# State times w_in of batches 4 to 7: from the first block into the second and third

## The chip, the cores and the metric

The kernel runs on one core of one Trainium2 chip. The metric is the device time of one execution in microseconds, the median of several runs. In the profile, PE is TensorE's matmuls, PEld its weight loads (which overlap the matmuls), DVE is VectorE, ACT is ScalarE, POOL is GpSimd, and SP is SyncE, which here only issues DMA transfers.

## The reference, cut to what matters

```python
def _attn_ref(x, state):                       # x 8 x 8 x 512 x 64, state 8 x 8 x 32 x 64
    a = softmax(scale * x @ state.T)           # over the 32 state rows
    xread = a @ state                          # 512 rows of each batch and head
    a2 = softmax(scale * state @ x.T)          # over the 512 tokens
    sread = a2 @ x                             # 32 rows of each batch and head
    return concat([xread, sread], axis=2)
# then, on 8 * 544 rows of 512 numbers:
h = x @ w_in                                   # 512 x 2048
x = max(0.01 * h, h) @ w_out                   # 2048 x 512
x = (silu(x @ w_gate) * (x @ w_val)) @ w_out2  # 512 x 1536, 1536 x 512
```

All in float32. The kernel gets the weights as 64-bit words (float64 bits) and converts them itself.

## The kernel before

**The trick of the first layer.** Since xread is a @ state, the product xread @ w_in is a @ (state @ w_in). The kernel therefore makes SW = state @ w_in once for every batch and head and multiplies the softmax weights a with it, which saves a step for the 512 token rows of a batch. The 32 sread rows of each batch are gathered in a "tail" that goes through w_in in the ordinary way at the end of the layer.

**Blocks and slots.** The first layer runs in eight blocks, one for each batch, of 16 slots each, one for each 128 columns of the hidden layer (variable `f`). The slots are numbered through: block j has slots 16 j to 16 j + 15. A steady slot has six matmuls into `ps_h` (`h_mm`, for the slot after next), the activation on ACT and DVE (`hs`, `gh`, `gl`), and twelve matmuls into four banks `ps_y` (`y_mm`). Every product of two float32 numbers is made from high and low parts in three passes (`passes`, line 443). After a block, `y_out` copies the four banks into one tile with the tag `yst` (128 x 4 x 512) and stores it.

**State times w_in before the change.** `product_sw(g, p, bs, banks)` makes, for column group g of w_in (4 of 512 columns), row group p (4 of 128 rows, two heads) and half bs of the batches (0 to 3, or 4 to 7), two matmuls over 64 rows each (line 467) into two banks. ACT copies each bank into a staging tile `sw` (line 475; two buffers for each of the two halves e) and SP stores it to `sw_dram` (line 476). There are 4 x 4 x 2 = 32 such calls, 64 matmuls (two records each in the trace), 64 copies and 64 stores of 256 KB. `load_sw` (line 494) loads the rows of one batch again, some slots before its block needs them, and `split_sw_h` and `split_sw_l` split them in high and low parts. Batch 0 alone is made straight from the banks (`state_win`, line 455, "keep").

**What sets the order in block 0.** Everything is issued in an order written out by hand: the string `START` ahead of slot 0, and one string of `SLOT0` for each slot of block 0. The letter `p` is one call of `product_sw` if some w_in piece is ready (`pump_products`, line 1187), `c` is one quarter of the conversion of one weight piece (`convert`: two ACT operations of lines 214 and 215, DVE operations of lines 216, 219, 222 and 225, one 512 KB load for the next piece; pieces of w_out are also split, lines 165 and 168, and pieces of w_in are stored in float32 to `win_dram`, line 232). `D`, `H`, `A`, `S`, `Y`, `L`, `Z` are the parts of the slot itself: H the matmuls into `ps_h`, Y and Z the two halves of `y_mm`. `finish1_h` forces products that are still open when the tile that holds their w_in piece is to be overwritten.

**Later blocks.** From slot 16 on, `put` lays each batch's softmax steps (`read_state`: scores into bank `a`; `read_tokens`: `turn` into bank `a`, `read` into bank `b`), the `load_sw` steps and the splits in the slots by their costs and due times. In a slot the parts run in the order W, D, matmuls, A, `y_mm`, and at last P and L of each step. The rest of a slot's vector time goes to `fill`, which converts the second layer's weights and stores their parts. Bank pool `ps_a` has one buffer for tag `a` and one for tag `b`. SP works through its DMAs in program order and waits at each one until its tile is free.

Of the kernel before, what the change touches and what calls it, by code (L numbers as in the profile page):

```python
# [9 lines left out]
F32 = mybir.dt.float32  # L10
# [15 lines left out]
def kernel(  # L26
# [46 lines left out]
    KD = DM // P  # L73
    NF1 = FF1 // P
    NF2 = FF2 // P
    NC = S // P
    NPAIR = H // 2
# [3 lines left out]
    FB = 4  # L81
# [6 lines left out]

    LOADS = "xswxxwww"
    ORDER = "iiiioiiooiioiioioiioioioiooooooo"  # L90
    START = "spc0Scpccc0p0cpccpcc1ccchcc1cccpc1clcpp0hcccpclp1c01cpcmcc"
    SLOT0 = [
        "DcHcpAccccSYLpcZccc",
        "DcHcAcccpSYLpccZccc",
        "DcHcpccAcSYLZccpp",
        "cDccHcApSccYLpcZcccc",
        "cDcHccApScYLcZpc",
        "cccDHpccAccScpYLccZ",
        "ccDcHAcpScccYcLZcp",
        "ccDccHcApSccpYcLcZ",  # L100
        "cDcHcpcApSYLcccZ",
        "ccDHcAScYcpLccZcp",
        "ccDcHcASYcpLccZcp",
        "cDHccASccYLcpcZ",
        "pcDHccASccYLcpcZ",
        "cpcDcHAccSYLccpccZp",
        "DcpcHcccpAcSYLcpZ",
        "pDpcHccpAcSYLcZp",
    ]
    KEEP = (0, 1, 3, 5, 8, 7)  # L110
    WS = 5

    Y_SUMS = 5

    WQ = 16

# [16 lines left out]
    first1 = layer1.enter_context(tc.tile_pool(name="first1", bufs=1))  # L133
    wsp = layer1.enter_context(tc.tile_pool(name="wsp", bufs=2))
    ab = layer1.enter_context(tc.tile_pool(name="ab", bufs=1))
    xin = layer1.enter_context(tc.tile_pool(name="xin", bufs=3))
# [9 lines left out]
    cv = first.enter_context(tc.tile_pool(name="cv", bufs=1))  # L146

    ident = const.tile([P, P], F32, name="ident")

    states = first1.tile([P, NPAIR, B, 2 * NS], F32, name="states")  # L150
    y_dram = [dram.tile([P, KD, widths[j]], F32, name=f"y_dram{j}") for j in range(NB)]
    win_dram = [dram.tile([P, KD, 512], F32, name=f"win_dram{g}") for g in range(FB)]

# [17 lines left out]
    xt, xn = {}, {}  # L171
# [18 lines left out]
    raw = {}  # L190
# [37 lines left out]
    ready = []  # L228
# [146 lines left out]
    def read_tokens(b, q):  # L375

        pairs = (2 * q, 2 * q + 1)
        v = {}

        def softmax_max():  # L380
            v["s"] = S_.pop((b, q))
            v["m2"] = at3.tile([P, 1], F32, tag="m2", name="m2")
            nc.vector.tensor_reduce(out=v["m2"], in_=v["s"], axis=AX.X, op=ALU.max)
            nc.vector.tensor_scalar(out=v["m2"], in0=v["m2"], scalar1=-SCALE, scalar2=None, op0=ALU.mult)

        def softmax_exp():
# [12 lines left out]
        def turn():  # L399
            ps = v["ps"] = ps_a.tile([P, 512], F32, tag="a", name="ps_a2")  # L400
            for c in range(NC):
                nc.tensor.transpose(ps[:, c * P:(c + 1) * P], v["e2"][:, c * P:(c + 1) * P], ident)

        def turned():
            v["et"] = at3.tile([P, 512], F32, tag="et", name="et")
            nc.scalar.copy(v["et"], v["ps"])

        def read():

            ps = v["ps"] = ps_a.tile([P, 2, NS], F32, tag="b", name="ps_r")  # L410
# [12 lines left out]
            next_xn(2)  # L423

        def read_out():
            nc.vector.tensor_copy(out=x_tail[:, pairs[0]:pairs[0] + 2, b * NS:(b + 1) * NS], in_=v["ps"])

        return [
            {"D": [softmax_max], "A": [softmax_exp], "cost": 0.8},
            {"D": [softmax_norm], "cost": 0.8},  # L430
            {"P": [turn], "L": [turned]},
            {"P": [read]},
            {"D": [read_out], "cost": 0.2},
        ]
# [14 lines left out]
    products = []  # L449
# [8 lines left out]
            )  # L458
        return ps

    def product_sw(g, p, bs, banks):

        pool = ps_y if banks == "yy" else ps_a
        ps = [pool.tile([P, 512], F32, tag=tag, name="ps_sw") for tag in banks]
        for e in range(2):
            half = slice(D * e, D * (e + 1))
            nc.tensor.matmul(  # L467
                ps[e], lhsT=flat[half, p, 4 * bs:4 * bs + 4, :].rearrange("d b n -> d (b n)"),
                rhs=raw["in", g, p][half], start=True, stop=True,
            )  # L470
        for e in range(2):

            pool, tag, bufs = ((cv, "sw", 2), (xin, "xn", 2))[e]
            t = pool.tile([P, 512], F32, tag=tag, name="sw", bufs=bufs)
            nc.scalar.copy(t, ps[e])  # L475
            nc.sync.dma_start(out=sw_dram[bs][g][2 * p + e], in_=t)

    def sw_tiles(b, g, q):
        SW[b, g, q] = tuple(wsp.tile([P, 512], F32R, tag="ab"[q] + t, name="sw" + t) for t in "hl")
# [8 lines left out]
        split_l(SW[0, g, q][1], sw_ps.pop((g, q)), SW[0, g, q][0])  # L488

    def load_sw(b, g, q):  # L490
        assert not any((g, p, b // 4) in products for p in (2 * q, 2 * q + 1))
        t = SW_raw[b, g, q] = xin.tile([P, 512], F32, tag="sw", name="sw")
        rows = slice(NS * (b % 4), NS * (b % 4 + 1))
        nc.sync.dma_start(
            out=t, in_=sw_dram[b // 4][g][4 * q:4 * q + 4, rows]
        )
# [8 lines left out]
    W = {}  # L505
# [500 lines left out]
    with tc.manual_schedule():  # L1006

        ins = [("in", g, k) for g in range(FB) for k in range(KD)]
        outs = [("out", f) for f in range(NF1)]
# [22 lines left out]
                raw[key] = cv.tile([P, 512], F32, tag="raw", name="raw", bufs=4)  # L1032

        def finish1_h(key):
            while any((KD * g + p) // 2 + NF1 // 2 == key[1] for g, p, _ in products):
                pump_products(1)
            t = wres.tile([P, 2, 512], F32R, tag=f"wr{key[1]}", name="w_parts")
            WO[key[1]] = (t[:, 0, :], t[:, 1, :])
            split_h(t[:, 0, :], raw[key])
# [84 lines left out]
        slots = {}  # L1124
# [7 lines left out]
        def put(start, steps, kind=None, behind=2):  # L1132


            at = []
            for k, step in enumerate(steps):
                slot = max([start] + [t + 1 for t in at[-1:] + before.get(kind, [])[k + behind:k + behind + 1]])
                cost = step.get("cost", 0)
                while k and "now" not in step and load.get(slot, 0) + cost > budget(slot):
                    slot += 1  # L1140
                load[slot] = load.get(slot, 0) + cost
                slots.setdefault(slot, []).append(step)
                at.append(slot)
            before[kind] = at
            return at

        def start_tokens(n):
            return NF1 + n * 11 // 2
# [18 lines left out]
        for g in range(1, FB):  # L1167
            for q in range(2):
                put(KEEP[2 * g - 2 + q], keep_steps(g, q), "keep")
        made = {0: 0, 1: 0}  # L1170

        for n in range(2, 2 * B):
            start = max((n // 2 - 1) * NF1 + EARLY + 6 * (n % 2), start_tokens(n - 4) + 1) if n > 3 else 6 * (n % 2)
# [1 line left out]
            made[n] = r[1] + 1  # L1175
            assert r[-1] < n // 2 * NF1 - 2, (n, r)
        for n in range(2 * B):
            put(max(start_tokens(n), made[n]), read_tokens(n // 2, n % 2), "tokens")

        def run(steps, part):  # L1180
            for step in steps:
                for op in step.get(part, ()):
                    op()

        products[:] = [(g, p, bs) for g in range(FB) for p in range(NPAIR) for bs in range(B // 4)]

        def pump_products(n, banks="ab"):
            for _ in range(n):
                one = next((one for one in products if ("in", *one[:2]) in ready), None)
                if one:  # L1190
                    products.remove(one)
                    product_sw(*one, banks)

        keep = [(0, 0), (0, 1)]
        low = list(keep)
# [2 lines left out]
        for action in LOADS:  # L1198
            if action == "w":
                next_load1()  # L1200
            elif action == "x":
                next_xt(1)
            else:
                nc.sync.dma_start(
                    out=flat.rearrange("p k b n -> p (k b n)"), in_=state_t.rearrange("e d k b n -> (e d) (k b n)")
                )
        nc.gpsimd.memset(states, 0.0)
        make_identity(nc, ident)

# [257 lines left out]
```

## Time and profile before

| | before |
|---|---|
| runs | 1481.33, 1483.01, 1483.09 us |
| median | 1483.01 us |
| profiled execution | 1480.25 us |
| its span | 1478.2 us |
| PE busy | 98% |
| PEld, DVE, ACT busy | 78%, 56%, 47% |
| HBM | 309.58 MB moved, 209 GB/s |
| block 0 ends (first copy of `yst`) | 155.35 us |
| first layer ends (last store of `yst`) | 702.7 us |

The profiled execution took 1480.25 us, 2.05 us more than its span and 2.76 us less than the median of the runs. The table is read from the top: PE is busy nearly always, and and the shares of the other engines are averages over stages with different limits: a first block in which the first layer's weights are converted and stored, seven blocks in which the second layer's are, and a second layer with no conversion. So the stretches are read apart below.

### The profile page before, as it was taken

To read this page: it belongs to the slowest core of one execution; us is meant where nothing else is said; L and a number is where in the kernel's file an instruction comes from. 1 tells how busy PE (TensorE), PEld (TensorE's weight loads), DVE (VectorE), ACT (ScalarE), POOL (GpSimd) and SP (SyncE) were. 2 spreads that over 40 slices of the span, in tenths; PEclk is the share of its full clock that TensorE was granted. 3 is DMA by queue.
4 is the path that set the end of the run, shared out by engine and by line. 5 is a ranking of instruction groups with operands and counts; after the bars stand their busy time and mean duration, and the time that the engine had idled before them with its cause. 6 is when DMAs were issued, how large, how long until landed. Compare 5 with 4: busy or idle time off the path is not lost.

```text
span 1478.2 us, 19617 instructions
## 1 busy us (share of the span) xinstructions
PE 1450.5 (98%) x7018; PEld 1159.7 (78%) x7018; DVE 829.4 (56%) x1460; ACT 688.2 (47%) x1242; POOL 3.0 (0%) x8
## 2 busy tenths in 40 slices
PE   5999999999999999999999999999999999999998
PEld 1545877878787878888888888888888878988887
DVE  5877677676767686243444535555344555644442
ACT  6877556655665666444333433334223333433322
POOL 0000000000000000000000000000000000000000
PEclk9999999999999999999999999999999999999999
DMA  8996556665655655260668676677666386876345
GB/s 296 317 321 217 186 206 214 206 223 191 228 214 198 207 189 200 90 208 21 215 194 280 229 233 203 193 220 244 232 193 193 104 309 228 266 255 193 119 150 191
DMA packets 146640, 309.58 MB, mean 209 GB/s; under 512 B 14064, under 2 KB 34544, under 8 KB 145520
## 3 DMA queue, kind: packets, MB, share of 16 engines
q1 hardware_dynamic: 145392, 299.95, 61.7%
q10 hardware_dynamic: 1152, 8.39, 1.4%
q8 instruction: 56, 0.92, 0.3%
q14 instruction: 40, 0.33, 0.1%
HBM read 231.74 MB, written 76.55 MB: 209 GB/s over the span
## 4 chain that ended last, share of the span: by engine, by line
PE 93%; DMA 3%; ACT 2%; DVE 1%; issue 1%; SPq 0%; ACTq 0%; DVEq 0%
PE ps_y L443 23%; PE ps_o L443 18%; PE ps_x L728 18%; PE ps_h L443 14%; PE ps_s L728 9%; PE ps_a L728 4%; PE ps_t L443 2%; PE ps_yt L443 2%; PE ps_sw L467 2%; PE ps_r L416 1%; PE ps_s L319 1%; DMA wo<-wo 1%; DMA wraw<-w_gate 1%; DMA sw_dram<-sw 1%; ACT sw L475 1%
## 5 line engine op out<-in xcount | busy, mean ns | idle before, releaser
L443 PE MATMUL ps_y<-gh,w_parts 128*128 128x512 f32 x1024 | 339.1, 391 | 0.0
L728 PE MATMUL ps_x<-yc,wq 128*128 128x512 f32 x1152 | 278.0, 389 | 0.0
L728 PEld LDWEIGHTS ps_x<-yc,wq 128*128 128x128 f32 x1152 | 216.2, 188 | 44.8
L443 PE MATMUL ps_o<-wo,zh 128*128 128x512 f32 x768 | 236.4, 389 | 0.0
L443 PEld LDWEIGHTS ps_y<-gh,w_parts 128*128 128x128 f32 x1024 | 192.2, 188 | 51.6 <-issue 7.6
L443 PE MATMUL ps_y<-gl,w_parts 128*128 128x512 f32 x512 | 199.3, 389 | 0.0
L168 DVE TENSOR_TENSOR gl<-hs,gh 128x512 fp32r<-128x512 f32 (+1 forms) x144 | 95.1, 660 | 146.9 <-ACT gh L165 146.7
L443 PEld LDWEIGHTS ps_o<-wo,zh 128*128 128x128 f32 x768 | 144.2, 188 | 30.0
L536 ACT ACTIVATE hs<-ps_h 128x512 f32<-128x512 f32 (+1 forms) x144 | 82.7, 575 | 180.2 <-PE ps_h L443 179.0
L443 PE MATMUL ps_o<-wo,zl 128*128 128x512 f32 x384 | 149.5, 389 | 2.0 <-DMA wo<-wo 2.0
L728 PE MATMUL ps_s<-yc,wq 128*128 128x512 f32 x576 | 146.1, 389 | 0.0
L168 DVE TENSOR_TENSOR zl<-z,zh 128x512 fp32r<-128x512 f32 x96 | 66.3, 691 | 117.4 <-ACT zh L165 117.4
L165 ACT CAST zh<-z 128x512 fp32r<-128x512 f32 x96 | 59.3, 621 | 143.6 <-PE ps_o L443 143.5
L728 PEld LDWEIGHTS ps_s<-yc,wq 128*128 128x128 f32 x576 | 108.1, 188 | 22.5
L748 ACT ACTIVATE sg<-C 128x512 f32<-128x512 f32 x72 | 45.5, 632 | 158.1 <-DVE C L744 158.1
L443 PEld LDWEIGHTS ps_y<-gl,w_parts 128*128 128x128 f32 x512 | 96.2, 188 | 19.6
L443 PE MATMUL ps_h<-ah,swl 128*128 128x512 f32 x256 | 106.6, 416 | 1.0 <-DVE swl L168 1.0
L744 DVE TENSOR_TENSOR C<-ps_s,C 128x512 f32<-128x512 f32 x48 | 33.2, 691 | 123.3 <-PE ps_s L728 123.3
L443 PE MATMUL ps_h<-al,swh 128*128 128x512 f32 x256 | 100.6, 393 | 0.1
L443 PE MATMUL ps_h<-ah,swh 128*128 128x512 f32 x256 | 100.7, 393 | 0.0
L740 ACT COPY C<-ps_x 128x512 f32<-128x512 f32 x96 | 56.1, 584 | 94.6 <-PE ps_x L728 93.8
L165 ACT CAST gh<-hs 128x512 fp32r<-128x512 f32 (+1 forms) x144 | 85.6, 595 | 3.0
(127 smaller groups left out, 1923.3 us busy)
## 6 DMA issues: line engine op xcount, KB each, us to landing
wo<-wo SPq DMA_DIRECT2D x96, 512.0 KB
wq<-quad_gate SPq DMA_DIRECT2D x168, 256.0 KB
wq<-quad_val SPq DMA_DIRECT2D x168, 256.0 KB
ws<-in_dram SPq DMA_DIRECT2D x68, 512.0 KB
sw_dram<-sw SPq DMA_DIRECT2D x64, 256.0 KB
sw<-sw_dram SPq DMA_DIRECT2D x56, 256.0 KB
quad_gate<-hl SPq DMA_DIRECT2D x24, 512.0 KB
quad_val<-hl SPq DMA_DIRECT2D x24, 512.0 KB
```

What stands on the lines that cost most here:

```text
L165: nc.scalar.copy(dst, src)
L168: nc.vector.tensor_tensor(out=dst, in0=src, in1=hi.bitcast(F32), op=ALU.subtract)
L319: nc.tensor.matmul(ps[2 * NS * i:2 * NS * (i + 1)], lhsT=states[:, p, b, :], rhs=xt.pop((b, p)), start=True, stop=True,)
L416: nc.tensor.matmul(ps[D * e:D * (e + 1), i], lhsT=tokens[i][:, c, D * e:D * (e + 1)], rhs=v["et"][:, n:n + NS], start=(c == 0), stop=(c == ...
L443: nc.tensor.matmul(ps, lhsT=w, rhs=v, start=first and n == 0, stop=last and n == len(todo) - 1)
L467: nc.tensor.matmul(ps[e], lhsT=flat[half, p, 4 * bs:4 * bs + 4, :].rearrange("d b n -> d (b n)"), rhs=raw["in", g, p][half], start=True, s ...
L475: nc.scalar.copy(t, ps[e])
L536: nc.scalar.activation(hs, ps[:, :n], AF.Prelu, alpha=0.01)
L728: nc.tensor.matmul(bank, lhsT=a, rhs=v, start=first and n == 0, stop=last and n == len(todo) - 1, skip_group_check=True,)
L740: nc.scalar.copy(t[0], src)
L744: nc.vector.tensor_tensor(out=kept[0], in0=bank, in1=kept[0], op=ALU.add)
L748: nc.scalar.activation(t[0], c, AF.Sigmoid)
```

## The change

Only the products of batches 0 to 3 stay in `START` and `SLOT0`: 16 of the 32 calls, and the letters `p` are thinned out accordingly (11 to 6 in `START`, 36 to 18 in `SLOT0`; the number of `c` is the same). The 16 products of batches 4 to 7 are made in eight rounds of two, four rounds in block 1 and four in block 2. A round takes three slots: in the first (part W) SP loads two 256 KB pieces of w_in from `win_dram` into a tile with the tag `yst`, the tile of the blocks' results; in the second and in the third slot one product each is made at the end of the slot (part P, ahead of the slot's other P steps, since it is inserted at place 0). ACT copies its two banks into the same tile, over the piece of w_in that was used, and SP stores from there. The rounds begin in slots 18, 21, 24, 27 and 34, 37, 40, 43. A new small tile `states1` holds the states of batches 4 to 7 and is loaded by one more DMA, issued from ACT, at the very start. (`held_b` comes out empty by the planner's own numbers, since `read_out` follows `read` in the next slot.)

```diff
-    def product_sw(g, p, bs, banks):
+    def product_sw(g, p, bs, banks, stationary, w, outs):
...
             nc.tensor.matmul(
-                ps[e], lhsT=flat[half, p, 4 * bs:4 * bs + 4, :].rearrange("d b n -> d (b n)"),
-                rhs=raw["in", g, p][half], start=True, stop=True,
+                ps[e], lhsT=stationary[half, p].rearrange("d b n -> d (b n)"), rhs=w[half], start=True, stop=True
             )
         for e in range(2):
...
+            t = outs(e)
             nc.scalar.copy(t, ps[e])
             nc.sync.dma_start(out=sw_dram[bs][g][2 * p + e], in_=t)
...
+    def later_sw(g, p):
+        v = {}
+        def begin():
+            v["t"] = ab.tile([P, KD, S], F32, tag="yst", name="later")
+            for i in range(2):
+                nc.sync.dma_start(out=v["t"][:, 2 * i, :], in_=win_dram[g][:, p + i, :])
+        def product(i):
+            product_sw(g, p + i, 1, "ab", states1, v["t"][:, 2 * i, :], lambda e: v["t"][:, 2 * i + e, :])
+        return [{"W": [begin]}, {"P": [lambda: product(0)]}, {"P": [lambda: product(1)]}]
...
+        for n in range(2 * FB):
+            slot = NF1 * (1 + n // 4) + LATER + 3 * (n % 4)
+            for step in later_sw(n // 2, 2 * (n % 2)):
+                while slot in held_b and "P" in step:
+                    slot += 1
+                slots.setdefault(slot, []).insert(0, step)
+                slot += 1
...
-        products[:] = [(g, p, bs) for g in range(FB) for p in range(NPAIR) for bs in range(B // 4)]
+        products[:] = [(g, p) for g in range(FB) for p in range(NPAIR)]
...
+        nc.scalar.dma_start(
+            out=states1.rearrange("p k b n -> p k (b n)"),
+            in_=state_t[:, :, :, 4:B, :].rearrange("e d k b n -> (e d) k (b n)"),
+        )
```

## Rows read from the trace of the kernel before

**Rows 1.** Windows: length, busy of PE, PEld, DVE, ACT, POOL; clock, DMA share, GB/s.

```profile
13.30:41.10 27.80, 23.49 (x58) 9.12 (x58) 22.26 (x44) 20.55 (x39) 0.00 (x0) 0.94 0.81 279
41.10:140.40 99.30, 93.27 (x344) 48.83 (x344) 81.01 (x154) 81.55 (x152) 0.00 (x0) 1.00 0.87 301
140.40:155.30 14.90, 14.90 (x67) 12.37 (x66) 4.76 (x8) 6.18 (x11) 0.00 (x0) 1.00 0.47 111
155.30:226.00 70.70, 70.70 (x376) 55.37 (x376) 49.41 (x99) 43.69 (x81) 0.00 (x0) 1.00 0.58 203
226.00:297.00 71.00, 71.00 (x393) 56.84 (x390) 50.60 (x104) 43.51 (x80) 0.00 (x0) 1.00 0.63 213
```

**Rows 2.** Chain that ended last, steady pieces: start us, us, what.

```profile
43.84 1.06 PE ps_sw L467 x4
44.90 1.59 PE ps_y L443 x6
...
170.36 0.44 PE ps_a L402 x4
...
174.90 1.06 PE ps_r L416 x32
...
184.34 1.36 PE ps_h L443 x6
185.70 2.72 PE ps_y L443 x12
```

**Rows 3.** Groups by line, 41.1 to 140.4: busy us, mean ns, idle before, releasers.

```profile
L467 PE MATMUL ps_sw<-w_in,flat 64*128 64x512 f32 x100 | 31.8, 641 | 4.3 <-ACT sw L475 4.3
L475 ACT COPY sw<-ps_sw 128x512 f32<-128x512 f32 x50 | 27.2, 591 | 6.7 <-PE ps_sw L467 3.7 <-DMA sw_dram<-sw 2.4 <-ACT hs L536 0.4
```

**Rows 4.** Waits of DVE, 41.1 to 140.4: us in total, times, longest.

```profile
DVE gl L168 <- ACT gh L165: 6.7, 4, 4.6
DVE w_in L216 <- ACT ws L214: 4.2, 4, 1.6
DVE swl L168 <- ACT swh L165: 3.6, 4, 1.5
```

**Rows 5.** Windows, two of the twelve slots 0 to 11; columns as in rows 1.

```profile
109.75:119.30 9.55, 8.37 (x33) 4.33 (x31) 4.20 (x8) 6.92 (x13) 0.00 (x0) 1.00 0.95 336
119.30:126.00 6.70, 6.70 (x29) 3.77 (x27) 6.70 (x14) 6.17 (x12) 0.00 (x0) 1.00 0.70 234
sum 104.40, PE 98.37 PEld 52.57 DVE 84.60 ACT 86.37 POOL 0.00; mean PE 8.20 PEld 4.38 DVE 7.05 ACT 7.20 POOL 0.00
```

**Rows 6.** Chain that ended last, DMA pieces: start us, us, what.

```profile
1.19 3.70 DMA flat<-in_dram
...
104.65 8.25 DMA sw_dram<-sw
```

**Rows 7.** Timeline of PE, 98 to 106: start, us, what [idle before <-releaser].

```profile
98.02 1.13 PE L467 MATMUL ps_sw<-w_in,flat 64*128 64x512 f32 x4
99.82 1.08 PE L319 MATMUL ps_s<-xt,states 128*64 128x512 f32 x4 [0.67 <-ACT sw L475]
...
102.43 1.13 PE L467 MATMUL ps_sw<-w_in,flat 64*128 64x512 f32 x4
104.23 1.61 PE L467 MATMUL ps_sw<-w_in,flat 64*128 64x512 f32 x4 [0.67 <-ACT sw L475]
105.77 0.50 PE L443 MATMUL ps_y<-gh,w_parts 128*128 128x512 f32 x1
```

**Rows 8.** Timeline of SP and ACT: a store and a reload, and who waited.

```profile
27.50 3.33 SPq L476 DMA_DIRECT2D sw_dram<-sw  x4
...
32.48 0.59 ACT L475 COPY sw<-ps_sw 128x512 f32<-128x512 f32 x1 [0.41 <-DMA sw_dram<-sw]
...
563.09 6.39 SPq L1260 DMA_DIRECT2D tail_in<-win_dram  x5
...
566.75 0.62 ACT L165 CAST ch<-tail_in 128x512 fp32r<-128x512 f32 x1 [2.19 <-DMA tail_in<-win_dram]
```

More of the change, by code (lines that the diff above doesn't have):

```diff
@@ L90 @@
     ORDER = "iiiioiiooiioiioioiioioioiooooooo"
-    START = "spc0Scpccc0p0cpccpcc1ccchcc1cccpc1clcpp0hcccpclp1c01cpcmcc"
+    START = "spc0Scccc0p0cccpcc1ccchcc1cccc1clcp0hcccpcl1c01cpcmcc"
     SLOT0 = [
[L93 to L103, printed above, removed]
+        "DcHcAccccSYLpcZccc",
+        "DcHcAcccSYLpccZccc",
+        "DcHcccAcSYLZccp",
+        "cDccHcApSccYLcZcccc",
+        "cDcHccApScYLcZc",
+        "cccDHpccAccScYLccZ",
+        "ccDcHAcpScccYcLZc",
+        "ccDccHcApSccYcLcZ",
+        "cDcHcpcASYLcccZ",
+        "ccDHcAScYcpLccZc",
+        "ccDcHcASYcpLccZc",
         "cDHccASccYLcpcZ",
[L105 to L108, printed above, removed]
+        "cDHccASccYLcpcZ",
+        "ccDcHAccSYLccpccZ",
+        "DcpcHcccAcSYLcpZ",
+        "DpcHccAcSYLcZp",
     ]
@@ L113 @@
     Y_SUMS = 5
+    LATER = 2
     WQ = 16
@@ L150 @@
     states = first1.tile([P, NPAIR, B, 2 * NS], F32, name="states")
+    states1 = first1.tile([P, NPAIR, B - 4, NS], F32, name="states1")
     y_dram = [dram.tile([P, KD, widths[j]], F32, name=f"y_dram{j}") for j in range(NB)]
@@ L467, in product_sw, with first_sw, staged_sw @@
             nc.tensor.matmul(
-                ps[e], lhsT=flat[half, p, 4 * bs:4 * bs + 4, :].rearrange("d b n -> d (b n)"),
-                rhs=raw["in", g, p][half], start=True, stop=True,
+                ps[e], lhsT=stationary[half, p].rearrange("d b n -> d (b n)"), rhs=w[half], start=True, stop=True
             )
         for e in range(2):
-            pool, tag, bufs = ((cv, "sw", 2), (xin, "xn", 2))[e]
-            t = pool.tile([P, 512], F32, tag=tag, name="sw", bufs=bufs)
+            t = outs(e)
             nc.scalar.copy(t, ps[e])
             nc.sync.dma_start(out=sw_dram[bs][g][2 * p + e], in_=t)
+    def first_sw(g, p, banks):
+        def staged_sw(e):
+            pool, tag, bufs = ((cv, "sw", 2), (xin, "xn", 2))[e]
+            return pool.tile([P, 512], F32, tag=tag, name="sw", bufs=bufs)
+        product_sw(g, p, 0, banks, flat[:, :, 0:4, :], raw["in", g, p], staged_sw)
+    def later_sw(g, p):
[7 more added lines that the diff above has]
+        return [{"W": [begin]}, {"P": [lambda: product(0)]}, {"P": [lambda: product(1)]}]
     def sw_tiles(b, g, q):
@@ L490, in load_sw @@
     def load_sw(b, g, q):
-        assert not any((g, p, b // 4) in products for p in (2 * q, 2 * q + 1))
+        assert b >= 4 or not any((g, p) in products for p in (2 * q, 2 * q + 1))
         t = SW_raw[b, g, q] = xin.tile([P, 512], F32, tag="sw", name="sw")
@@ L1034, in finish1_h @@
         def finish1_h(key):
-            while any((KD * g + p) // 2 + NF1 // 2 == key[1] for g, p, _ in products):
+            while any((KD * g + p) // 2 + NF1 // 2 == key[1] for g, p in products):
                 pump_products(1)
@@ L1169 @@
                 put(KEEP[2 * g - 2 + q], keep_steps(g, q), "keep")
-        made = {0: 0, 1: 0}
+        made, held_b = {0: 0, 1: 0}, set()
         for n in range(2, 2 * B):
@@ L1177 @@
         for n in range(2 * B):
-            put(max(start_tokens(n), made[n]), read_tokens(n // 2, n % 2), "tokens")
+            at = put(max(start_tokens(n), made[n]), read_tokens(n // 2, n % 2), "tokens")
+            held_b.update(range(at[3] + 1, at[4]))
+        for n in range(2 * FB):
[5 more added lines that the diff above has]
+                slot += 1
         def run(steps, part):
@@ L1183, in run @@
                     op()
-        products[:] = [(g, p, bs) for g in range(FB) for p in range(NPAIR) for bs in range(B // 4)]
+        products[:] = [(g, p) for g in range(FB) for p in range(NPAIR)]
         def pump_products(n, banks="ab"):
             for _ in range(n):
-                one = next((one for one in products if ("in", *one[:2]) in ready), None)
+                one = next((one for one in products if ("in", *one) in ready), None)
                 if one:
                     products.remove(one)
-                    product_sw(*one, banks)
+                    first_sw(*one, banks)
         keep = [(0, 0), (0, 1)]
```

## The prediction, made before the change was run

> **What bounds the kernel now.** I first cut the span in stretches, busy time of each engine [rows 1]. From 155.3 us on, in blocks 1 and 2, PE is busy in all of 70.7 and 71.0 us, with ACT at 62% and DMA at about 60%: whatever is added to PE there lengthens the span by its full time. Block 0 looks different: from 41.1 to 140.4 us, its slots 0 to 11, PE is busy 93.27 of 99.30 us, ACT 81.55, DVE 81.01, DMA 87%. Nothing is at its limit by itself, three are near. Then I read the chain of waits for the price of a product [rows 2], the groups by line for how many lie where [rows 3], and DVE's waits for how much of its idle time is the products' doing [rows 4]. Slots 12 to 15 (140.4 to 155.3 us) hold no product any more and run at PE's pace, so they don't change.
>
> **Products on PE.** In the chain one product (four records) takes 1.06 us, and the six matmuls after it 1.59 instead of the 1.36 that six take in the steady state [rows 2]: 1.06 + 0.22 = 1.28 us of PE for each. The sixteen products in blocks 1 and 2 therefore cost 16 x 1.28 = 20.5 us. In eight of the sixteen places another float32 step (scores, turn or read) follows in the same slot, and the 0.22 is paid there already: -1.8. Term: **+18.7 us**, bounds 17.0 (no 0.22 anywhere) to 20.5.
>
> **What block 0 gives back.** Of the 32 products 25 lie in slots 0 to 11 (100 records [rows 3]) and 7 before them, where PE waits for the first conversions anyway. After the change 4 fit in `START` by its letters and 12 in the slots: 13 fewer, or 13 x 1.28 = 16.6 us of PE, and the waits that ACT's copies cause, 4.3 us [rows 3], mostly go too. PE alone could give some 21 to 25 us. But the number of `c` is unchanged, and so is DVE's work: 84.6 us in the twelve windows of the slots from 36 us on, which last 104.4 us [rows 5]. So DVE is late next. I took for each slot the larger of DVE's busy time in its window and PE's new work (4.08 from rows 2, plus 1.28 for one product, plus 1.01 + 0.22 where a keep or scores step lies in it). That is DVE in eleven of the twelve (the last row with DVE at 6.70 of 6.70 us is one) and PE in slot 8 (9.55 us now, 6.6 then), and sums to 87.1. At 96%, a little under what DVE reaches in slot 9 alone, that is 90.7 us, 13.7 less than now. Term: **-14 us**. Bounds: -20 (DVE without any pause, 84.6) to -7: of DVE's 18.3 us of idle time in slots 0 to 11 the waits for `gh`, `ws` and `swh` are 14.5 [rows 4], and half of them, those on `swh` among them, are chains of PE, ACT and DVE that remain. What hides nothing here: the stores that go (16 products, 8.4 MB) free DMA, which isn't the bound then, and the 32 copies of 0.59 us [rows 3] free ACT, which has room by then.
>
> **The start.** The load of `states1` (256 KB) goes in beside the load of `flat`, 512 KB in 3.70 us, which ACT's first copy waits for [rows 6]. Half as much again could delay that by 0 to 1.9 us; three fewer products before 41 us take ACT's copies out of a stretch where DVE is busy 22.26 of 27.80 us [rows 1], a gain of 0 to 2. I take **+0.4 us**. Its issue on ACT lies in the time in which ACT waits for `flat`.
>
> **Waits for a bank.** A product takes banks `a` and `b` at the end of a slot, ahead of the slot's other P steps, and these need the same banks, of which there is one each. The trace has both cases [rows 7]: scores behind a product started 1.80 us after it instead of 1.06, so +0.74 for bank `a`; and a second product, whose second half needs `b`, took 1.54 instead of 1.06 on top, so +1.22 for `b`. Going through the plan by its costs and due times, a product stands ahead of scores or turn (`a`) in slots 22, 23, 28, 29 and 45 and ahead of read (`b`) in slots 19, 35 and 41. Term: 5 x 0.74 + 3 x 1.22 = **+7.4 us**, bounds 4 (copies that start at once) to 10 (ACT late by 0.3 us each time). Behind the waiting matmul PE's whole next slot is queued.
>
> **Waits for the reload.** The tile with tag `yst` has one buffer. So each round's two loads wait on SP until the four stores of the round before have landed, and the second product's stores are issued only at the end of the slot just before. From the start of a second product at t: the copies end and the store is issued at t + 2.2 (102.43 to 104.65 [rows 6, 7]); a 256 KB store of this kind landed 4.9 us after its issue (27.50 to 32.44, by the copy that waited [rows 8]), in another place 8.25 [rows 6]; a 256 KB load from the very same `win_dram` took 3.7 (563.09 to 566.75 [rows 8]). The next product can start at t + 2.2 + 4.9 + 0.1 + 3.7 = t + 10.9. PE is there at t + 1.28 + 2 x 4.08 = t + 9.4, later where P steps lie between (turn 0.44, scores 1.2, read 1.3 [rows 2]). For the six rounds that follow on another in their block that gives waits of 1.5, 0, 1.5, 1.5, 1.0 and 0.2. Term: **+5.7 us**. Bounds: 0.6 (a store as fast as the load, 3.7) to 24.8 (8.25 for the store). I take 4.9, since DMA is at 60% in blocks 1 and 2 against 81% in the stretch of the 4.9 [rows 1]; the 8.25 fell where it was at 87%.
>
> By the Trainium skill, DMA: Bandwidth & Descriptors, section Anatomy of one DMA, a transfer costs about 2.0 us fixed and its bytes at 436 GB/s; an estimate from that page is 2.6 us for 256 KB. By it the reload would be there at t + 7.5, the waits would be nil and the sum 5.7 lower; the two rows, 3.7 and 4.9, speak against it, since neither queue was empty.
>
> What is queued behind the waiting load on SP: the loads of `ws`, `xt`, `xn` and `sw` and the stores of the second layer's parts. They come up to 7 us later, six times; ACT and DVE have 38% and 30% of idle time there [rows 1], `load_sw` has three slots until its split, so I cost that at nothing. If that cover is gone (DVE held up ahead of `gl`), it is one slot's 4 us.
>
> **The sum.** -14 + 18.7 + 0.4 + 7.4 + 5.7 = +18.2 us. On the profiled execution, 1480.25 us, that is 1498.5; the median of the runs stands 2.8 higher, so **1501 us**.
>
> **Rivals.**
> *Faster: block 0 falls to PE's floor.* If DVE's pieces of work can move ahead into the time that ACT and the stores now hold up, PE's own work bounds slots 0 to 11: 12 x 4.08 + 12 x 1.28 + eight keep and scores steps at 1.23 = 74.2 instead of 99.3, a gain of 25, and with a reload that is always in time and copies that never keep a bank, +18.7 only: 1477 us. It decides if block 0 shrinks by more than what the waits leave, 26 us with bank waits and 19 without. Against it: DVE has 81.0 us of work in those 99.3 [rows 1], 7 more than PE's floor. For it: the many short waits of DVE on ACT [rows 4]. Chance 0.07.
> By the Trainium skill, Perfetto Trace Analysis, section Optimization Strategy, a kernel whose most-contended engine changes may gain if its regimes are interleaved; this rival is that rule, and the rows bear it out for ACT and DMA, which have room in blocks 1 and 2, not for PE, which has none.
> *About the same.* Block 0 gives 20, the reload is in time, and the bank waits are at 4: -20 + 18.7 + 4 = +2.7, 1486 us. For it: DVE at 100% in slot 9. Chance 0.10, of which I put 0.07 within the bound.
> *Much slower: the store and reload become the bound.* At 8.25 us for a store [rows 6] the reload waits are 24.8 instead of 5.7: 1520 us. It decides from t + 9.4 on. Against it: DMA isn't that full there. For it: `sw`, `ws` and `hl` transfers stand ahead in the same queue. Chance 0.15.
> *Block 0 hardly shrinks.* Only -7, since PE, ACT and DVE hand work to each other slot by slot: 1508 us. Chance 0.13.
> That the change doesn't do what it says I leave out: all 32 products have to be made in either version.
>
> **How the numbers follow.** The forecast, 1501 us, has 0.55; its own range is 1493 to 1510. For 8 in 10 the range reaches from 1486 (the middle of "about the same") to 1516: left out are the faster rival (0.07), a part of the case beside it (0.04) and the longer half of the reload rival (0.08). Faster by over 0.2% (3 us, about what a measurement of this kernel can tell from no change): 0.07. Within 0.2%: 0.07. Slower: 0.86.
>
> **What would show it.** Right: block 0's first copy of `yst` some 14 us earlier than 155.35 us, with DVE over 90% busy in slots 0 to 11 and PE less; blocks 1 and 2 some 15 us longer each than 71, where PE shows waits on ACT `sw` and on a DMA into the tile `later`, and from block 3 on nothing changed. Wrong: a block 0 that ends 25 us earlier; no idle time of PE in blocks 1 and 2; waits for the reload over 3 us a round, or waits of PE on `gl` there.

## The result and the profile after

The changed kernel takes 1503.14 us, the median of runs from 1502.83 to 1504.86, against 1482.47 us before (1481.33 to 1483.09; four runs, of which the table above had three). The ratio is 1.0138, with an interval of 1.0121 to 1.0155: slower by some 20 us. Its profiled execution took 1502.83 us with a span of 1501.0 us, 22.8 us more than the span before. All ratios here and below are of fast runs, which leaves out a single execution of 3897 us in the last experiment.

Where a block ends is seen by its first copy into `yst`, here in the timeline of ACT (start, us, instruction):

```profile
142.92 2.15 ACT L600 COPY yst<-ps_y 128x512 f32<-128x512 f32 x4
233.51 2.01 ACT L600 COPY yst<-ps_y 128x512 f32<-128x512 f32 x4
325.88 2.04 ACT L600 COPY yst<-ps_y 128x512 f32<-128x512 f32 x4
397.59 2.04 ACT L600 COPY yst<-ps_y 128x512 f32<-128x512 f32 x4
```

| stretch | before, us | after, us | difference |
|---|---|---|---|
| block 0, to the first copy | 155.35 | 142.92 | -12.4 |
| block 1 | 74.80 | 90.59 | +15.8 |
| block 2 | 72.96 | 92.37 | +19.4 |
| block 3 | 71.72 | 71.71 | 0.0 |
| from there to the end of the span | 1103.37 | 1103.41 | 0.0 |

The whole of the difference lies in the first three blocks: -12.4 + 15.8 + 19.4 = +22.8 us.

The windows of after answer to [rows 1] (length, busy of PE, PEld, DVE, ACT, POOL, then clock, DMA share and GB/s); 41.1 to 128.0 are the slots that hold products, and then blocks 1 and 2:

```profile
41.10:128.00 86.90, 77.85 (x298) 44.78 (x297) 76.93 (x147) 68.59 (x125) 0.00 (x0) 1.00 0.78 261
142.90:233.50 90.60, 84.91 (x444) 61.00 (x443) 52.77 (x105) 54.89 (x101) 0.00 (x0) 1.00 0.70 236
233.50:325.90 92.40, 85.93 (x438) 62.48 (x437) 51.03 (x104) 51.89 (x97) 0.00 (x0) 0.96 0.69 232
```

Block 0's slots lost 15.4 us of PE's work and 12.4 us of length. DVE is now busy 89% of them (82% before) and PE 90% (94% before). DVE has the same work in block 0 in both; 3.5 us of it moved behind the last product, to slots 12 to 15 (8.26 us there, 4.76 before). In blocks 1 and 2 PE was busy without a pause before; now it sits idle for 5.7 and 6.5 us, and in block 2 the granted clock is below 1. What PE waited for there, by the view of waits from 142.9 to 325.9 us (total us, times, longest):

```profile
PE ps_r L420 <- ACT later L476: 4.8, 3, 2.5
PE ps_sw L471 <- DMA later<-win_dram: 3.8, 3, 2.1
PE ps_a L406 <- ACT later L476: 2.1, 3, 0.7
PE ps_s L323 <- ACT later L476: 1.4, 2, 0.7
```

Three rows are waits for a bank that ACT still copies to `later`, one is the wait for the reload.

In block 0's slots PE's waits changed hands. Before, 5.0 us of them were for ACT's copies of `sw` (4.3 of them the products' [rows 3]) and 1.0 us for DVE; in after 8.1 us are for DVE. First before, from 41.1 to 140.4 us, then the two largest of after, from 41.1 to 128 us:

```profile
PE ps_h L443 <- DVE swl L168: 1.0, 2, 0.5
...
PE ps_sw L459 <- DVE w_in L229: 4.7, 2, 3.2
PE ps_sw L471 <- DVE swl L172: 1.8, 1, 1.8
```

DVE's own waits in these slots, which answer to [rows 4]; the first line is one of before that stands beside them, the others are of after:

```profile
DVE raw L216 <- ACT ws L214: 2.2, 4, 0.8
...
DVE gl L172 <- ACT gh L169: 3.7, 4, 1.2
DVE swl L172 <- ACT swh L169: 2.6, 2, 1.4
DVE raw L220 <- ACT ws L218: 2.5, 2, 2.2
DVE w_in L220 <- ACT ws L218: 1.2, 2, 0.7
```

With that line, before has 14.5 + 2.2 = 16.7 us of waits for `gh`, `ws` and `swh`; after keeps 3.7 + 2.6 + 2.5 + 1.2 = 10.0.

### The profile page after: what moved, and what is told of

It reads as the page before. It is cut to its first block, busy times and chain, and to the rows that moved or that the text cites. A ratio compares the mean times of both kernels' runs of the same rounds, so it can differ in the third digit from the quotient of the medians.

```text
span 1501.0 us, 19629 instructions
## 1 busy us (share of the span) xinstructions
PE 1451.8 (97%) x7018; PEld 1159.9 (77%) x7018; DVE 828.8 (55%) x1460; ACT 689.0 (46%) x1242; POOL 3.0 (0%) x8
## 4 chain that ended last, share of the span: by engine, by line
PE 90%; DMA 3%; DVE 3%; ACT 2%; issue 1%; SPq 0%; ACTq 0%; DVEq 0%
PE ps_y L447 21%; PE ps_o L447 18%; PE ps_x L752 17%; PE ps_h L447 13%; PE ps_s L752 9%; PE ps_a L752 4%; PE ps_t L447 2%; PE ps_sw L471 2%; PE ps_yt L447 2%; DMA sw_dram<-later 1%; PE ps_r L420 1%; PE ps_s L323 1%; DMA ws<-in_dram 1%; ACT later L476 1%; DMA later<-win_dram 0%
```

## The experiments

### Block 0 without the rounds

Theory: the gain of block 0 and the price of blocks 1 and 2 are independent and add up. Rival: block 0's earlier end is paid for by something later, so that without the rounds part of it comes back.

```diff
-        for n in range(2 * FB):
+        for n in range(0):
...
-            out=t, in_=sw_dram[b // 4][g][4 * q:4 * q + 4, rows]
+            out=t, in_=sw_dram[0][g][4 * q:4 * q + 4, rows]
```

> The changed kernel without its eight rounds: the sixteen products of batches 4 to 7 are left out, and these batches read the products of batches 0 to 3. Theory (block 0 gives 12.4 us by itself, and the 35.2 us that blocks 1 and 2 got longer are the rounds' alone): block 0 ends at 142.9 us as in the changed kernel, blocks 1 and 2 take 74.8 and 73.0 us as before, total 1503.1 - 35.2 = 1468 us. Rival (block 0 only handed on work, transfers or late loads to block 1, which would make it longer without any round): blocks 1 and 2 stay above 150 us together, total over 1472 us.

Measured: 1471.75 us, ratio 0.9923 (0.9894 to 0.9953). Block 0 ended at 143.10 us, and blocks 1, 2 and 3 took 74.80, 72.96 and 71.72 us, those of before to the hundredth. So block 0's gain stays, nothing in the later blocks hangs on it, and the rounds alone cost the 35.2 us. The total is 3.8 us above the 1468 expected, and most of that lies elsewhere: what follows block 7's first copy, mostly the second layer, took 783.8 us here and 780.8 in before. Its instructions are the same in all versions, and over the executions profiled here it took 780.7 to 783.9 us. So the blocks are compared below, and the totals only roughly.

### The rounds without the reload

Here the products take their 64 rows from a resident tile, so that no load of `later` is made and its tile is waited for by nothing but its own stores.

```diff
         def begin():
             v["t"] = ab.tile([P, KD, S], F32, tag="yst", name="later")
-            for i in range(2):
-                nc.sync.dma_start(out=v["t"][:, 2 * i, :], in_=win_dram[g][:, p + i, :])
...
-            product_sw(g, p + i, 1, "ab", states1, v["t"][:, 2 * i, :], lambda e: ...)
+            product_sw(g, p + i, 1, "ab", states1, WO[0][0].bitcast(F32), lambda e: ...)
```

> The changed kernel, where the sixteen later products take a w_out part that is in SBUF anyway instead of w_in read back: the sixteen loads are left out, the matmuls, copies and stores stay. Theory (the reload costs its waits on PE, 3.8 us, and through SP's queue the late store that held ACT and then PE, 1.3 us, and the stretch at half clock behind it, 3.6 us): 8.7 us less, 1494 us. Rival 1 (only the waits seen on PE): 3.8 less, 1499 us. Rival 2 (other waits take their place, since PE is late anyway): 1 us less or nothing, 1502 to 1503 us.

Measured: 1500.13 us, ratio 1.0118 (1.0093 to 1.0144); blocks 1 and 2 took 88.55 and 86.02 us, 8.4 less than in after. Block 0 ended 2.0 us later than in after with the same instructions (granted clock 0.91 from 100 to 120 us, 1.00 in after), and the second layer was 1.6 us longer, which hides part of the gain in the total. The window of blocks 1 and 2 and PE's waits in them:

```profile
144.90:319.50 174.60, 167.78 (x880) 121.10 (x879) 103.78 (x208) 106.86 (x197) 0.00 (x0) 1.00 0.63 221
PE ps_r L420 <- ACT later L476: 3.5, 3, 1.2
PE ps_a L406 <- ACT later L476: 2.0, 3, 0.7
PE ps_s L323 <- ACT later L476: 1.3, 2, 0.7
```

That parts the 35.2 us. PE is idle for 174.60 - 167.78 = 6.8 us, all of it bank waits. Against 147.76 us before, the two blocks took 26.8 more, so the products themselves are 26.8 - 6.8 = 20.0 us, 1.25 each. The reload, with all that hangs on it, is the remaining 8.4.

Only 3.8 of those 8.4 are waits for the load. The rest shows in block 2 of after, in the timelines of SP, ACT and PE (in brackets, the idle time before the instruction and its releaser):

```profile
276.72 0.81 SPq L477 DMA_DIRECT2D sw_dram<-later  x2
283.31 0.80 SPq L494 DMA_DIRECT2D later<-win_dram  x2
284.22 0.36 SPq L1133 DMA_DIRECT2D quad_val<-hl  x1
...
286.98 1.13 PE L471 MATMUL ps_sw<-later,states 64*128 64x512 f32 x4 [2.07 <-DMA later<-win_dram]
288.98 0.62 ACT L169 CAST hl<-two 128x512 fp32r<-128x512 f32 x1 [3.85 <-DMA quad_val<-hl]
289.50 1.07 ACT L476 COPY later<-ps_sw 128x512 f32<-128x512 f32 x2
290.62 1.92 PE L420 MATMUL ps_r<-et,xn 128*64 128x32 f32 x32 [2.51 <-ACT later L476]
```

SP stands at the round's load until the stores have landed, from 276.7 to 283.3 us. Behind that load is the store of a second-layer part from `hl`, which leaves at 284.2. ACT needs that `hl` tile for its next cast and waits 3.85 us. ACT's copies of the product's banks come after that cast, so the read that needs bank `b` waits 2.51 us instead of the 1.2 it waits in the version without the reload, which has no wait of ACT on these stores. And then PE's clock falls. Windows of after around it, columns as above:

```profile
284.00:287.00 3.00, 0.93 (x7) 0.46 (x5) 2.23 (x4) 1.13 (x2) 0.00 (x0) 1.00 0.77 211
287.00:290.00 3.00, 1.11 (x4) 0.28 (x4) 0.00 (x0) 1.02 (x3) 0.00 (x0) 1.00 1.04 421
290.00:294.00 4.00, 3.38 (x36) 3.03 (x37) 2.10 (x4) 1.08 (x3) 0.00 (x0) 0.51 0.79 265
294.00:298.00 4.00, 4.00 (x13) 3.16 (x12) 1.04 (x3) 1.80 (x3) 0.00 (x0) 0.64 0.68 192
```

PE was busy 2.04 of 6 us, and in the next eight the granted clock is 0.51 and 0.64, that is, mostly the level of 1.2 GHz. At full clock the same work would have taken (1 - 0.51) x 4 + (1 - 0.64) x 4 = 3.4 us less, at most. So the 8.4 are 3.8 of direct waits, 1.3 of a read that waits for a late ACT, and, as an estimate from these two windows, about 3.4 of half clock. No run has the stall without the half clock, so the last part is worked out and not parted by an experiment.

### The products in slots where no step shares their banks

The bank waits fall away if the products lie in slots without scores, turn or read. The list gives for each round the slot of the load and those of the products; it reaches into block 3.

```diff
+        FREE = [(18, 20, 21), (23, 25, 26), (34, 36, 37), (38, 39, 42), (43, 44, 47), (49, 50, 53), (54, 55, 58), (59, 60, 61)]
         for n in range(2 * FB):
-            slot = NF1 * (1 + n // 4) + LATER + 3 * (n % 4)
-            for step in later_sw(n // 2, 2 * (n % 2)):
...
+            for slot, step in zip(FREE[n], later_sw(n // 2, 2 * (n % 2))):
```

> The changed kernel with the same eight rounds, begun in slots 18, 23, 34, 38, 43, 49, 54, 59 and their products in slots in which no scores, turn or read step follows (20, 21, 25, 26, 36, 37, 39, 42, 44, 47, 50, 53, 55, 58, 60, 61). Theory (bank waits cost some 7 to 8 us of idle PE, a product by itself 1.28 us): no wait of PE on ACT's copies of the tile later is left, four of the eight reloads are as tight as before, so 1503.1 - 8 - 3 = 1492 us, between 1489 and 1496. Rival (the products cost 35.2 / 16 = 2.2 us each wherever they stand, since PE changes its kind of matmul twice): 1503 us, with blocks 1 to 3 longer by 2.2 us for each product.

Measured: 1502.9 us, ratio 1.014 (1.0115 to 1.0164), a miss by 11 us. The bank waits are gone, as expected; PE's waits from block 1 to block 3 hold only these two, and the first is new:

```profile
PE ps_y L447 <- ACT yst L600: 7.3, 1, 7.3
PE ps_sw L471 <- DMA later<-win_dram: 0.3, 1, 0.3
...
317.50 2.05 ACT L600 COPY yst<-ps_y 128x512 f32<-128x512 f32 x4 [7.13 <-DMA sw_dram<-later]
317.00:323.00 6.00, 4.87 (x12) 3.80 (x13) 1.34 (x3) 4.20 (x8) 0.00 (x0) 0.50 0.44 180
```

A product in slot 47, the last of block 2, has its results in the very tile into which `y_out` wants to copy the block's results in slot 48. ACT waits 7.13 us for the stores, PE 7.3 us for ACT's copies of its banks, and after that PE runs at a clock of 0.50. My expectation had counted the waits between rounds and forgotten the tile's first owner. The other 4.8 us lie in block 0, whose instructions are those of after: it ended at 147.69 us with half-clock stretches, one of them from 76 to 81 us (clock 0.70, 1.00 in after).

### The same with the last product out of the way

```diff
-        FREE = [..., (43, 44, 47), ...]
+        FREE = [..., (43, 44, 45), ...]
```

> As the run with products in free slots, but the product of slot 47 stands in slot 45, so that its store has landed when the block's results want the same tile at slot 48. Theory (a product by itself costs PE 1.28 us; what was left in that run was the wait of 7.3 us for the tile and the stretch at half clock behind it): blocks 1, 2 and 3 take 74.8 + 4 x 1.3, 73.0 + 6 x 1.3 and 71.7 + 6 x 1.3 us and at most 2 us more for one bank wait and tight reloads; total about 1494 us. Rival (moving the products cannot be had below the changed kernel's time, since other waits fill in): 1500 us or more.

Measured: 1494.97 us, ratio 1.0077 (1.0051 to 1.0103); blocks 1, 2 and 3 took 80.01, 81.59 and 81.31 us. PE's waits in all three:

```profile
PE ps_a L406 <- ACT later L476: 0.7, 1, 0.7
PE ps_sw L471 <- DMA later<-win_dram: 0.4, 2, 0.2
```

So the waits can be had for 1.1 us in all, and the reload and bank terms together were nearly all a matter of the slots chosen. What can't be had for less is PE's time: four products in block 1 cost 5.21 us, 1.30 each; over the three blocks it is 23.4 us less the waits, 1.39 each. Part of the 23.4 is only a moved mark: ACT makes the copy that ends block 3 after a wait of 1.20 us, and block 4, which has no product, is 1.3 us shorter than before (72.32 us against 73.60). To the end of block 4 it is 22.1 us, and less the waits 1.31 each, near the 1.28 of the prediction. Against -12.4 us in block 0 even the cleanest place loses.

### The reload and its stores on GpSimd's queue

If SP's order is what holds up the `hl` stores, another queue should take that away.

```diff
-            nc.sync.dma_start(out=sw_dram[bs][g][2 * p + e], in_=t)
+            (nc.gpsimd if bs else nc.sync).dma_start(out=sw_dram[bs][g][2 * p + e], in_=t)
...
-                nc.sync.dma_start(out=v["t"][:, 2 * i, :], in_=win_dram[g][:, p + i, :])
+                nc.gpsimd.dma_start(out=v["t"][:, 2 * i, :], in_=win_dram[g][:, p + i, :])
```

> The changed kernel with the rounds' loads and stores issued from GpSimd's queue instead of SP's; SP's own order is as before the change. Theory (the waiting load on SP holds up the second layer's stores behind it, and these ACT's and PE's work): ACT's waits on the quad stores, 6.4 us in blocks 1 and 2, and the stretch at half clock are gone, PE's own wait for the reload stays: 1503.1 - 5 = 1498 us. Rival (SP's queue hid it all; only the reload's own time counts): 1503 us, or more if GpSimd issues a transfer later than SP does.

Measured: 1523.64 us, ratio 1.0268 (1.0232 to 1.0304), a miss by 26 us. ACT's waits on `quad_val` and `quad_gate`, 4.1 and 2.6 us in after, are gone, and the read waits 1.2 us each time, so SP's order was indeed their cause. But the reload itself is much later. PE's waits in blocks 1 and 2, and the row of DMA issues (count, size, median us to landing):

```profile
PE ps_sw L471 <- DMA later<-win_dram: 15.1, 6, 4.4
PE ps_r L420 <- ACT later L476: 3.5, 3, 1.2
...
later<-win_dram POOLq DMA_DIRECT2D x16, 256.0 KB, 5.1
```

A load took 5.1 us from issue to landing, against 3.2 and 3.6 us for two of SP's loads in after's chain. The six rounds that follow on another in their block now all wait, up to 4.4 us. Blocks 1 and 2 took 96.67 and 99.25 us, 13.0 more than in after; the other 7 us of the total lie in block 0, 4.1 us longer with the same instructions, and in the second layer. So the time is near that of the rival "the store and reload become the bound" (1520 us), but only two thirds of the way there are the reload's. By the Trainium skill, DMA: Bandwidth & Descriptors, section Issuing engines are not separate DMA queues, issuing from several engines only saves the time of issuing, since all transfers run on the same DMA engines; in these rows the time to landing was longer too. Whether GpSimd's queue or the transfers beside it made it so, no run here shows.

### What bounds block 0: DVE's work taken away

In `convert` one DVE operation of each piece, the clamp of the converted numbers, is left out while block 0 runs, once in after and once in before. Theory: after is bound by DVE, before by PE.

```diff
-            if prev:
+            if prev and not finish:
                 prev["limit"]()
```

> The changed kernel, where the first layer's conversions leave out one of DVE's operations (the clamp, 0.42 us, 32 times; no input here reaches the clamp). Theory (with half of the products gone DVE bounds block 0): DVE has 13.4 us less to do, some 10.6 of it in slots 0 to 11, and block 0 ends 7 to 10 us earlier, up to where PE's work is the bound; total about 1495 us. Rival (ACT, the loads or PE bound block 0): 2 us less or nothing, 1501 us or more.

> The kernel before, where the first layer's conversions leave out the same operation of DVE. Theory (before the change PE, with its products, and DVE share the bound, PE in most slots): block 0 ends 2 to 4 us earlier, total about 1479 us. Rival (DVE bounded block 0 all along): 7 to 10 us earlier, total 1474 us.

Measured, after without it: 1499.02 us, ratio to before 1.0092 (1.0074 to 1.0109), block 0 at 140.09 us, 2.8 earlier. Before without it: 1483.22 us, ratio 0.999 (0.9979 to 1.0), block 0 at 157.83 us, 2.5 later. Both theories missed in size: they had 7 to 10 us and 2 to 4 us earlier. The windows of the slots with products, first of after, then of before without the clamps:

```profile
41.10:126.00 84.90, 78.39 (x293) 45.19 (x292) 69.58 (x124) 67.46 (x124) 0.00 (x0) 0.98 0.78 264
...
41.10:140.40 99.30, 93.25 (x337) 49.11 (x335) 71.26 (x125) 79.94 (x149) 0.00 (x0) 0.97 0.84 293
```

In before, DVE's work fell from 81.01 us [rows 1] to 71.26, and PE kept both its work (93.25) and its 4.3 us of waits on `sw`. Block 0 didn't end earlier; its clock was 0.84 from 100 to 120 us (1.00 in before), which costs at most 3.2 us, so that at full clock it would have ended some 1 us earlier than before, no more. DVE was not the bound there. In after, some 10 us of DVE's work are worth 2.8 us, or at most 4.6 with the clock of 0.91 from 60 to 80 us taken out. So DVE is on the path in after, and it isn't alone on it. In the waits of after without the clamps, from 41.1 to 126 us, DVE waits on ACT:

```profile
DVE raw L220 <- ACT ws L218: 4.7, 5, 2.7
DVE w_in L220 <- ACT ws L218: 4.2, 4, 2.2
```

With 3.5 us for `swh` and 2.7 for `gh` that is 15.1 us, against 10.0 in after: of the time that DVE gained it spends some 5 us behind ACT.

### The other half of the products taken away too

Without the sixteen products that after leaves in block 0, and without the rounds:

```diff
-                    first_sw(*one, banks)
+                    pass
```

> The changed kernel without any product by 64 rows: the rounds are left out, and so are the sixteen products of block 0 with their copies and stores; the later blocks load as many bytes of x in their place. Theory (DVE bounds block 0, so a second half of the products brings much less than the first half's 12.4 us): block 0 ends 2 to 5 us before 143 us, total about 1465 us. Rival (PE bounds it still): 12 x 1.28 = 15 us earlier, block 0 ends at 128 us, total 1454 us.

Measured: 1462.54 us, ratio 0.9845 (0.9825 to 0.9865), block 0 at 136.26 us. The first sixteen gave 12.4 us, these sixteen 6.8, counted from the 143.10 us of the version without rounds. PE's waits and the window of its slots:

```profile
PE ps_sw L459 <- DVE w_in L229: 7.1, 4, 2.7
PE ps_y L447 <- DVE w_parts L172: 4.4, 4, 1.9
...
41.10:121.00 79.90, 66.39 (x232) 42.16 (x231) 70.96 (x139) 52.15 (x94) 0.00 (x0) 0.89 0.62 201
```

With no such product left PE is busy 83% and ACT 65% of the slots and PE waits 11.5 us for DVE's conversions; DVE is at 89%, as in after. So the second half gave about half of what the first gave, and it is DVE that PE then waits for, though DVE isn't full even then. The size is not clean: the clock was 0.89 in this window and 1.00 in after, which is up to 8.8 us of PE's time, and how much of that lengthened block 0 no run shows. By its time alone the rival (15 us) isn't excluded; the waits speak against it.

### Eight products moved instead of sixteen

The letters of before stay, and half as many products move, in four rounds in block 1.

```diff
-        for n in range(2 * FB):
+        for n in range(FB):
...
-        products[:] = [(g, p) for g in range(FB) for p in range(NPAIR)]
+        products[:] = [(g, p, bs) for g in range(FB) for p in range(NPAIR) for bs in range(2 if g >= 2 else 1)]
```

> Half of the change: the hand-written order of before with its letters, the four rounds of block 1 as in the changed kernel, and the eight products of batches 4 to 7 with the second half of w_in's columns in block 0. Theory (what block 0 gives back falls with each product that goes, since PE is the bound at first and DVE's conversions are later): block 0 ends 8 to 10 us earlier than 155.35, block 1 is 15 to 16 us longer, total about 1489 us. Rival (each product gives the same 12.4 / 16 = 0.78 us): 6 us earlier, total 1492 us. In either case slower than before.

Measured: 1502.13 us, ratio 1.0119 (1.0097 to 1.0141), a miss by 13 us. Blocks 1 to 3 took 88.99, 72.96 and 71.72 us, so eight products cost 14.2 us there, but block 0 ended at 159.61 us, 4.3 later than before. The largest of PE's waits from 36 to 155 us, which before doesn't have:

```profile
PE ps_sw L471 <- DVE w_in L229: 6.4, 2, 3.5
```

By the order of the letters, with those of before and fewer products, a `p` comes to the piece that the `c` just ahead of it converts, and PE stands there for 6.4 us in two waits. There is also one wait of 4.5 us for `al`, ended at 36.5 us, which before doesn't have either, and the clock was 0.83 from 60 to 80 us (1.00 in before). So this run suggests that the letters have to be thinned together with the products, and it says nothing on how block 0's gain falls from product to product. That stays open.

### Products parted from the steps that need their banks, in before

The bank waits are the one cost that the kernel before has as well: 4.3 us on `sw` [rows 3], seen at 99.82 and 104.23 us [rows 7]. In four slots the second of two products that stand one behind the other moves to between the two halves of `y_mm`; then, in a fifth slot, a product right ahead of the scores too. Nothing else is changed.

```diff
-        "DcHcpccAcSYLZccpp",
+        "DcHcpccAcSYpLZccp",
...
-        "cccDHpccAccScpYLccZ",
-        "ccDcHAcpScccYcLZcp",
-        "ccDccHcApSccpYcLcZ",
-        "cDcHcpcApSYLcccZ",
+        "cccDHpccAccScpYLccZ",
+        "ccDcHAcpScccYcpLZc",
+        "ccDccHcApSccYpcLcZ",
+        "cDcHcpcASYpLcccZ",
```

> The kernel before, where in four slots of block 0 (2, 5, 7 and 8) the second of two products that stand one behind the other is moved between the two halves of the slot's result matmuls; all 32 products stay in block 0. Theory (what the change rightly takes away in block 0 is mostly PE waiting at such pairs for ACT's copies, 4.3 us): about 4 us less than before, 1478 us. Rival (DVE or ACT take the place of these waits): within 1.5 us of before.

> The kernel before, with the pairs of products parted in slots 2, 5, 7 and 8 as in the earlier run, and in slot 6 the product at its end, which held up the scores by 1.24 us, moved between the two halves of the slot's result matmuls. Theory (PE is the bound of block 0, and its waits on ACT's copies are what can be saved there): 2 to 3.5 us less than before, 1480 us. Rival (block 0 has no time to give, since DVE fills in): within 1.5 us of before.

Measured: four slots (without the third line) 1480.84 us, ratio 0.9983 (0.997 to 0.9997), block 0 at 153.57 us; five slots 1481.39 us, ratio 0.9975 (0.9963 to 0.9987), block 0 at 154.05 us. The timeline of PE at the place of [rows 7], with five:

```profile
98.96 1.08 PE L319 MATMUL ps_s<-xt,states 128*64 128x512 f32 x4 [0.27 <-ACT sw L475]
...
104.20 1.33 PE L467 MATMUL ps_sw<-w_in,flat 64*128 64x512 f32 x4
```

The scores wait 0.27 us instead of 0.67, and the product at 104.20 has no wait ahead of it. By the medians this version is faster than both kernels, by 0.25% of before, measured beside it; before itself had medians from 1481.80 to 1485.81 us in the four sets of runs. The trace shows less. PE's waits for the copies of `sw` fell from 5.0 to 1.2 us, but block 0 is only 1.3 us shorter, which is within the rival's 1.5, and its start up to 41.1 us ran at a clock of 1.00 here and 0.96 in before, worth up to 1.6 us by itself. The profiled execution is not shorter in all (1481.63 us against 1480.25), since the second layer took 2.6 us more. So what the parting is worth stays open.

## Why the prediction was right, and where it was not

The forecast was 1501 us, the time is 1503.14. The products, the bank waits and the reload waits were right in mechanism, block 0's by half, and one path, which was put at nothing, was wrong. That the sum came so near is in part luck, since two misses in block 0 offset each other. Term by term:

**Block 0, with the start: right in size, half right in its reason.** -13.6 us forecast, -12.4 measured. "So DVE is late next" is true only in part. PE does wait for DVE there now, but DVE's share rose to 89% and not over 90%; some 10 us of its work are worth 2.8 us; with all the products gone it still stands at 89%. The step that took for each slot the larger of DVE's time and PE's work and then stretched the sum by 4% put in for one engine what is a chain of three: ACT's first step, DVE's second and PE's use of it, with waits in each direction. The size came out by luck, because two misses offset each other: DVE is idle for 10.0 us of these slots, where the forecast had left 90.7 - 84.6 = 6.1, and it is busy for 76.93 us in them against 81.01 before, where I had left its work as it was; most of the difference moved to slots 12 to 15. The faster rival, which needed 19 to 26 us, is refuted by the 12.4.

**Products on PE: slightly too low.** 18.7 forecast, 20.0 measured. At 1.25 us each the price of [rows 2] holds; the 1.8 that I took off for switches shared with a following float32 step was too much. In the chain of the version without the reload, where a read or scores follows, the product takes 1.11 us and the step 0.06 or 0.07 more than without a product ahead of it, and where turn follows, turn takes 0.66 instead of 0.44.

**Bank waits: right.** 7.4 forecast, 6.8 measured. Three reads of bank `b` at 1.2 us each and five steps on bank `a` at 0.66 us, against 1.22 and 0.74. The difference is a reading of two views at once: the 1.80 us is from the timeline, which starts this product at 98.02, and the 1.06 from the chain, which starts it 0.07 later. In before's chain alone:

```profile
98.09 1.11 PE ps_sw L467 x4
...
99.82 1.08 PE ps_s L319 x4
```

That is 1.73 - 1.06 = 0.67 for bank `a`, 1.15 for `b`, and 5 x 0.67 + 3 x 1.15 = 6.8, as measured.

**Reload waits: the direct part smaller than forecast, three waits instead of five.** 5.7 forecast, 3.8 measured. The chain shows two reloads that PE waited for, with longer stores than the 4.9 us that I took and shorter loads than the 3.7 (in the next round 5.15 and 3.17 us):

```profile
189.00 6.28 DMA sw_dram<-later
195.40 3.57 DMA later<-win_dram
```

By the Trainium skill, DMA: Bandwidth & Descriptors, section Anatomy of one DMA, the estimate had been 2.6 us for 256 KB; none of these four is as short. The page gives its figure for transfers that GpSimd issues, and these are SP's.

**What is queued behind SP's waiting load: the step that failed.** I costed it at nothing, and added: "If that cover is gone (DVE held up ahead of `gl`), it is one slot's 4 us". It cost 8.4 - 3.8 = 4.6 us, but not by the path that I named, DVE held up ahead of `gl`; that this is near those 4 us is chance. I had looked at the loads that come late and at the shares of idle time of ACT and DVE, which are averages. What was late was a store that had to free a tile for ACT; ACT's copy of the product's bank stood behind it in ACT's own order, and PE behind that. And the idle PE then lost its clock, which no term had.

**The rest held.** Sum of the terms forecast 18.2 us, measured 22.8 between the profiled executions and 20.7 between the medians: the profiled execution of before lies 2.2 us under its median, that of after at its own. From block 3 on nothing changed, to some hundredths of a microsecond in these two executions. "About the same" failed on block 0 (12.4 us instead of 20), on the reload and on the bank waits; "much slower" came near only on the other queue; "block 0 hardly shrinks" is refuted by 12.4 us.

## What to carry to other kernels

Work that is moved out of a stage where several engines are near their limit gives less than its full price, and into a stage where its own engine has no pause it costs all of it: here 12.4 us against 20.0, before any wait. A tile that is borrowed brings its owner's due times with it, and a load that waits for it holds up everything behind it in its queue; of those transfers, look first at the stores that free a tile. Waits for banks and reloads can be placed away (the choice of slots alone took 35.2 us down to 22.1), so when a move loses, ask first what it costs with all of them gone.

## What the runs showed of the hardware beyond that

The granted clock matters in sums of a few microseconds. It was 0.51 after 2.04 us of work in 6, and 0.50 after a wait of 7.3 us. But PE's pauses alone don't decide it. Block 0 has the same work in after, without the rounds, without the reload, with free slots and with GpSimd's queue, and ended at 142.92, 143.10, 144.90, 147.69 and 147.00 us. In two of them PE, DVE and ACT did the same, to 0.2 us, in each window of 5 us from 56 to 76 us, with the clock at 1.00. In the next one the clock differs, and with it the number of matmuls that PE finished (after, then free slots):

```profile
76.00:81.00 5.00, 5.00 (x20) 3.41 (x19) 4.96 (x10) 4.04 (x8) 0.00 (x0) 1.00 1.01 352
...
76.00:81.00 5.00, 4.98 (x13) 3.43 (x14) 4.96 (x10) 4.17 (x8) 0.00 (x0) 0.70 1.01 354
```

Why the clock fell in the second, no run here shows. So a block in which PE has many short pauses has a spread of its own, 4.8 us here, while block 3, where it holds no product, has no pause and repeats to 0.01 us. A comparison block by block shows that at once; the totals don't.
